# Lightning attention into a PReLU feed-forward: another hand-written list for the stretch ahead of the loop

## The chip, the cores and the metric

The kernel runs on one core of a Trainium2 chip. The metric is the time of one execution on the device, in microseconds (us), as the median of several runs. PE is TensorE (PEld its weight loads), DVE is VectorE, ACT is ScalarE, POOL is GpSimd, and SP issues most of the DMA transfers.

## What is computed

Block attention with a decaying state, per batch and head, and a feed-forward layer with a PReLU behind it. In the reference, cut to what matters:

```python
# q, k, v: (4, 8, 768, 64); lam: (8,); w_in: (512, 2048); w_out: (2048, 512); alpha: (2048,)
for b in range(nb):                       # blocks of 64 rows
    intra = (qb @ kb.T * Dmask) @ vb      # Dmask[i, j] = lam**(i - j) for i >= j, else 0
    inter = (qb * lam**(i + 1)) @ kv_state
    out[b] = intra + inter
    kv_state = lam**64 * kv_state + (kb * lam**(63 - i)).T @ vb
x = out as (3072, 512)
h = x @ w_in
g = max(h, 0) + alpha * min(h, 0)
y = g @ w_out                             # (3072, 512), float32
```

## The kernel before

**Tiles.** The kernel uses blocks of 128 rows, two of them at a time (a window of 256 rows). A *chunk* `c` of 0 to 5 is one window of two batches: chunk 0 is the first window of batches 0 and 1, chunk 1 the first window of batches 2 and 3, chunk 2 the second window of batches 0 and 1, and so on. A chunk has four *units*, numbered through from 0 to 23: unit `4c + 2 bi + hh` is batch `bi` of the chunk and four of the eight heads (`hh`). Each unit's state depends on that of the unit eight numbers before it, which has the same batch and heads, so units of one chunk are independent of each other.

**What a unit needs.** Its k, q and v arrive in float32 (`load`, issued on SP; chunk 0 in 256 KB halves of heads, later chunks in 512 KB). `cast` makes float16 copies, on ACT ("A"), DVE ("V") or POOL ("G"). `key_decayed` makes keys times decay. q and k are transposed, either on PE with a copy from PSUM behind it (`transposed` for one of the two, `transposes` for both with one copy of 1024 elements), or by a DMA transpose (`transposes(..., "D")`, issued on SP). `decayed` multiplies transposed queries by decay; in the first two chunks only the second block needs it.

**Clusters.** `cluster(old, new)` issues on PE: the state part of unit `old` (L361), the scores of unit `new` (L378), the masked scores times v of `old` (L390) and the state products of `new` (L405). Then DVE makes the masked scores of `new` (`sm`, L416), the outputs of `old` are copied into `xT` (the feed-forward's input), and the states of `new` are written: for the first block by ACT (L436, L437), for others by DVE (`R`, L440). From chunk 2 on POOL copies states into a block-diagonal tile `RD` (L454), which L361 reads. Outputs and state products share the one PSUM tile `acc` (two banks).

**Feed-forward.** `up(c, f)` computes one of 16 slices of h for a chunk (four matmuls of 512 columns, L465), then ACT makes relu(-h) (L473, tile `m`) and DVE the sum g (L489). With `bi` given it does half a chunk. `down(c, t, part, 4)` does a quarter of the 16 matmuls of an output tile (L502); behind the last quarter, ACT copies the tile (L515) and SP stores it (L518). The PSUM banks are `acc` (2), the scores `s0`, `s1` (1 each), and four that `up`, `down`, `fill` and PE transposes share under the tags "h" (a ring of two), "op" and "tk".

**Weights.** `load_win(i)` and `load_wout(i)` fetch the weights of 512 of the 2048 hidden columns each (four slices f); they are issued on POOL's queue, in its order. `gate(i, which)` is a one-element DMA on SP that reads from a weight piece, so SP issues nothing further until that piece has landed.

**Order.** Nothing is scheduled by the compiler: each engine runs what the program issues to it in the order of issue. Up to the loop this order is a list written out call by call (L573 to L788). `fill(n, bank)` issues n matmuls whose result nobody reads. From L790 on, the loop weaves `up(c)` and `down(c - 1)` for chunks 2 to 5 with the attention of the next chunk, and `down_last` ends the kernel.

Of the kernel before, what the change touches and what calls it, by code (L numbers as in the profile page):

```python
# [11 lines left out]
def kernel(  # L12
# [16 lines left out]
    nc = tc.nc  # L29
# [85 lines left out]
    def zero_states(batches, eng):  # L115
        for b in batches:
            for hh in (1, 0):
                eng.memset(RD[b, hh].bitcast(fp32), 0.0)
# [227 lines left out]
    def cluster(old, new, eng="A"):  # L346
# [5 lines left out]
        kv = [acc[:, a, 256:384].rearrange("p (h d) -> p h d", h=2) for a in range(2)]  # L352
        if old is not None:
            co, bo, ho = units[old]
            pbo, bb = co // 2, 2 * (co % 2) + bo
            to = T[old]
            for a in range(2):
                if 2 * pbo + a == 0:
                    continue
                for hp in range(2):  # L360
                    nc.tensor.matmul(  # L361
                        ot[a][:, hp, :].rearrange("p (e j) -> p e j", e=2),
                        lhsT=RD[bb, ho][:, a, hp].rearrange("p h d -> p (h d)"),
                        rhs=to["qdT"][:, :, hp, ds(a * 64, 64)],
                        start=(hp == 0),
                        stop=False,
                        skip_group_check=True,
                    )
# [29 lines left out]
        if new is not None:  # L398
            kv_of = [a for a in range(2) if 2 * pb + a + 1 < S // L]
            for hp in range(2):  # L400
                for e in range(2):
                    for hl in range(2):
                        for a in kv_of:
                            p = ds(a * 64, 64)
                            nc.tensor.matmul(  # L405
                                kv[a][ds(hl * 64, 64), hp, :],
                                lhsT=t["kdec"][p, e, 2 * hp + hl, :],
                                rhs=t["v16"][p, e, 2 * hp + hl, :],
                                start=(old is None and hp == 0 and e == 0),
                                stop=(e == 1),  # L410
                                skip_group_check=True,
                            )
# [7 lines left out]
        if old is not None:  # L420
# [8 lines left out]
        if new is not None:  # L429
            for a in kv_of:  # L430
                n = 2 * pb + a
                then = R[b, hh, n + 1]
                if n == 0:
# [3 lines left out]
                    nc.scalar.activation(then, kv[a], AF.Copy)  # L437
                    continue
                for hp in range(2):
                    nc.vector.scalar_tensor_tensor(  # L440
                        out=then[:, hp],
# [54 lines left out]
    def down(c, t, part, nparts, bank="op"):  # L496
# [12 lines left out]
        if part == nparts - 1:  # L509
            store(c, t, o_ps, 0, DM)  # L510
            del O[c, t]

    def store(c, t, o_ps, c0, n):
# [4 lines left out]
        nc.sync.dma_start(out=rows, in_=o_sb[:, 0:n])  # L518
# [53 lines left out]

    mask_logs(1)  # L573
    mask_logs(2)
    decay_mask(1)
    mask_logs(0)
    load(0, 0, "k", 0)
    load(0, 0, "q", 0)
    query_decay(2, 1)
    load(0, 0, "v", 0)  # L580
    load(0, 0, "k", 1)
    cast(0, "q16", "V")
    query_decay(0, 1)
    key_decay()
    key_decayed(1, "G")
    key_decayed(0, "G")
    mask_logs(3)
    query_decay(3, 1)
    cast(0, "v16", "A")
    decay_mask(3)  # L590
    cast(0, "k16", "V")
    fill(9, "h")
    transposed(0, 1, "V", "tk")
    cast(1, "k16", "A")
    fill(3, "h")
    transposed(1, 1, "V", "h")
    load(0, 0, "q", 1)
    cast(1, "q16", "A")
    transposed(0, 0, "V", "op")
    load(0, 0, "v", 1)  # L600
    query_decay(1, 1)
    decayed(0, "V")
    load(0, 1, "k", 0)
    load(0, 1, "q", 0)
    load(0, 1, "v", 0)
    cast(1, "v16", "G")
    state_decay()
    load(0, 1, "k", 1)
    decay_mask(0)
    fill(3, "tk")  # L610
    cluster(None, 0)
    slopes()
    transposed(1, 0, "V", "h")
    load_win(0)
    cast(2, "q16", "A")
    fill(5, "tk")
    transposed(2, 0, "V", "op")
    load(0, 1, "q", 1)
    cast(2, "k16", "A")
    cast(3, "k16", "V")  # L620
    load(0, 1, "v", 1)
    decay_mask(2)
    cluster(0, 1, "A")
    fill(4, "tk")
    transposed(3, 1, "V", "op")
    transposed(2, 1, "A", "tk")
    key_decayed(3, "V")
    load_win(1)
    key_decayed(2, "G")
    cast(3, "q16", "A")  # L630
    decayed(1, "G")
    fill(3, "h")
    cluster(1, None, "A")
    gate(1, "in")
    load(1, 0, "k", None)
    load(1, 0, "q", None)
    cast(2, "v16", "V")
    load(1, 0, "v", None)
    cluster(None, 2)
    transposed(3, 0, "A", "op")  # L640
    decayed(3, "V")
    cast(3, "v16", "V")
    decayed(2, "G")
    fill(4, "h")
    cluster(2, 3, "A")
    up(0, 0, 0, "tk")
    load_win(2)
    load_win(3)
    up(0, 1, 0, "h")
    fill(2, "op")  # L650
    cluster(3, None, "A")
    up(0, 5, 0, "h")
    up(0, 5, 1, "op")
    up(0, 3, None, "tk")
    up(0, 0, 1, "h")
    up(0, 2, None, "op")
    query_decay(3, 0)
    cast(4, "k16", "G")
    up(0, 6, None, "h")
    up(0, 9, None, "h")  # L660
    key_decayed(4, "G")
    up(0, 4, None, "tk")
    up(0, 1, 1, "op")
    up(0, 7, None, "h")
    transposed(4, 1, "V", "h")
    cast(5, "q16", "A")
    up(0, 14, None, "tk")
    transposed(5, 0, "A", "h")
    cast(4, "q16", "G")
    transposed(4, 0, "V", "h")  # L670
    gate(3, "in")
    load(1, 1, "k", None)
    load(1, 1, "q", None)
    cast(5, "k16", "G")
    decayed(5, "G")
    cast(4, "v16", "A")
    up(0, 12, None, "op")
    up(0, 8, None, "tk")
    load(1, 1, "v", None)
    up(0, 11, 0, "h")  # L680
    load_wout(0)
    cast(6, "k16", "A")
    up(0, 11, 1, "h")
    load_wout(1)
    gate(1, "out")
    key_decayed(5, "G")
    cast(7, "k16", "G")
    up(0, 15, None, "op")
    cluster(None, 4)
    load(2, 0, "k", None)  # L690
    load(2, 0, "q", None)
    load(2, 0, "v", None)
    load(2, 1, "k", None)
    transposed(5, 1, "A", "tk")
    cast(6, "q16", "A")
    up(0, 10, None, "h")
    up(0, 13, None, "tk")
    transposed(6, 1, "V", "h")
    transposed(6, 0, "A", "op")
    cast(5, "v16", "G")  # L700
    decayed(4, "G")
    cluster(4, 5, "A")
    transposed(7, 1, "V", "h")
    cast(7, "q16", "G")
    transposed(7, 0, "A", "op")
    down(0, 2, 0, 4, "tk")
    down(0, 3, 0, 4, "h")
    down(0, 0, 0, 4, "op")
    load_wout(2)
    key_decayed(6, "V")  # L710
    load_wout(3)
    decayed(6, "V")
    key_decayed(7, "G")
    query_decay(2, 0)
    cast(6, "v16", "A")
    cluster(5, 6, "A")
    cast(7, "v16", "A")
    down(0, 2, 1, 4, "tk")
    down(0, 0, 1, 4, "op")
    cast(9, "k16", "G")  # L720
    decayed(7, "V")
    down(0, 3, 1, 4, "h")
    cast(8, "q16", "G")
    cast(8, "v16", "G")
    cluster(6, 7, "A")
    cast(8, "k16", "V")
    transposes(8, "D", False)
    key_decayed(8, "V")
    down(0, 2, 2, 4, "tk")
    cast(11, "k16", "G")  # L730
    key_decayed(9, "G")
    load(2, 1, "q", None)
    load(2, 1, "v", None)
    down(0, 0, 2, 4, "op")
    query_decay(1, 0)
    key_decayed(10, "G")
    cluster(7, None, "A")
    cast(9, "q16", "G")
    transposes(9, "D", False)
    down(0, 3, 2, 4, "h")  # L740
    down(0, 3, 3, 4, "h")
    up(1, 12, None, "h")
    up(1, 1, None, "h")
    down(0, 0, 3, 4, "op")
    query_decay(0, 0)
    decayed(8, "G")
    up(1, 0, None, "h")
    up(1, 8, None, "h")
    down(0, 2, 3, 4, "tk")
    cast(10, "k16", "A")  # L750
    cluster(None, 8)
    up(1, 11, None, "op")
    cast(10, "q16", "A")
    up(1, 14, None, "tk")
    up(1, 13, None, "h")
    transposes(10, "D", False)
    up(1, 6, None, "h")
    down(0, 1, 0, 4, "op")
    decayed(9, "G")
    cast(9, "v16", "A")  # L760
    cast(11, "q16", "G")
    transposes(11, "D", False)
    cluster(8, 9, "V")
    up(1, 7, None, "h")
    key_decayed(11, "G")
    cast(11, "v16", "A")
    decayed(10, "G")
    down(0, 1, 1, 4, "op")
    down(0, 1, 2, 4, "op")
    cast(10, "v16", "A")  # L770
    cluster(9, 10, "V")
    load(3, 0, "k", None)
    up(1, 5, None, "tk")
    load(3, 0, "q", None)
    load(3, 0, "v", None)
    decayed(11, "G")
    up(1, 9, None, "h")
    down(0, 1, 3, 4, "op")
    load(3, 1, "k", None)
    load(3, 1, "q", None)  # L780
    load(3, 1, "v", None)
    cluster(10, 11, "V")
    up(1, 3, None, "tk")
    up(1, 2, None, "h")
    up(1, 15, None, "h")
    up(1, 4, None, "op")
    cluster(11, None, "A")
    up(1, 10, None, "tk")  # L788
# [42 lines left out]
```

## Time and profile before

| what | value |
|---|---|
| three runs | 219.31, 220.54, 218.2 us; median 219.31 |
| the profiled execution | 220.27 us, its span 218.5 us |
| PE busy | 207.5 us (95%) |
| DVE, ACT, POOL busy | 131.0, 115.8, 91.0 us |
| granted clock of PE | 0.997 on the mean |
| read from and written to HBM | 27.27 and 6.29 MB |

The span is the time between the first and the last instruction of the profiled execution. An engine's busy time is the sum over the time in which it ran an instruction; waiting, and issuing of DMA transfers on SP, are not busy. Idle time of an engine matters only where something else waits for what it does next. Durations used below are those of this one execution.

### The profile page before, as it was taken

The numbers are of one execution on the slowest core, as the hardware profiler recorded it, in microseconds if no ns is written. First come the engines' busy times: TensorE is split into PE (matmuls) and PEld (weight loads), VectorE is DVE, ScalarE is ACT, GpSimd is POOL, SyncE is SP. The second block draws the span as 40 slices with busy tenths as digits, with TensorE's granted clock in tenths as the row PEclk, the third lists the DMA queues.
The fourth block names the chain that finished last, engine by engine and source line by source line (L and its number), as shares of the span: only waits on it lengthen the run. The fifth ranks groups of instructions, "written<-read, shape, count | busy, mean of one in ns | idle before, by whom it ended". The sixth has DMA issues, their size and how long they took to land.

```text
span 218.5 us, 5235 instructions
## 1 busy us (share of the span) xinstructions
PE 207.5 (95%) x2087; PEld 105.9 (48%) x2087; DVE 131.0 (60%) x259; ACT 115.8 (53%) x224; POOL 91.0 (42%) x165
## 2 busy tenths in 40 slices
PE   7888999999898999999999999999999999999993
PEld 2445555644354544555545544554545444444453
DVE  7798688964697964866855646546645444444000
ACT  6876679764663575365456445545435434444121
POOL 5590059402587573697693484375331000000000
PEclk9999999999999999999999999999999999999998
DMA  5999999999899999689656997242111011110212
GB/s 151 295 245 189 264 290 217 165 228 242 201 270 197 308 234 212 160 211 240 168 123 193 155 237 221 55 99 65 33 51 48 0 51 50 48 48 3 96 48 96
DMA packets 62478, 33.90 MB, mean 155 GB/s; under 512 B 18150, under 2 KB 59510, under 8 KB 62454
## 3 DMA queue, kind: packets, MB, share of 16 engines
q1 hardware_dynamic: 58182, 29.37, 53.3%
q0 software_dynamic: 4224, 4.19, 12.3%
q8 instruction: 16, 0.26, 0.5%
q14 instruction: 8, 0.07, 0.1%
q10 hardware_dynamic: 48, 0.01, 0.0%
HBM read 27.27 MB, written 6.29 MB: 154 GB/s over the span
## 4 chain that ended last, share of the span: by engine, by line
PE 75%; DMA 12%; POOL 3%; SPq 3%; ACT 2%; issue 1%; DVE 1%; ACTq 0%; POOLq 0%
PE h_ps L465 34%; PE o_ps L502 27%; PE o_ps L525 6%; DMA w_out_sb<-in_moe_w_out_dram 6%; DMA qkT<-qk 4%; SPq L87 3%; PE s L378 3%; DMA kraw<-in_k_dram 3%; PE acc L390 2%; PE acc L361 2%; PE acc L405 1%; POOL w_out_sb L102 1%; POOL qk L248 1%; ACT xT L244 1%; ACT m L473 1%
## 5 line engine op out<-in xcount | busy, mean ns | idle before, releaser
L489 DVE SCALAR_TENSOR_TENSOR g<-m,oma,h_ps 128x512 f16<-128x512 f32 (+1 forms) x100 | 71.7, 725 | 59.1 <-ACT m L473 57.7
L465 PE MATMUL h_ps<-xT,w_in_sb 128*128 128x512 f16 (+1 forms) x400 | 95.6, 371 | 0.3 <-ACT qkT L244 0.3
L473 ACT ACTIVATE m<-h_ps 128x512 f32<-128x512 f32 (+1 forms) x100 | 57.5, 579 | 63.7 <-PE h_ps L465 62.2
L502 PE MATMUL o_ps<-w_out_sb,g 128*128 128x512 f16 x320 | 81.3, 380 | 0.3 <-DMA w_out_sb<-in_moe_w_out_dram 0.3
L465 PEld LDWEIGHTS <-w_in_sb 128*128 128x128 f16 x400 | 38.1, 98 | 42.0 <-issue 0.6
L502 PEld LDWEIGHTS <-g 128*128 128x128 f16 x320 | 30.3, 98 | 35.7 <-issue 0.6
L454 POOL COPY RD<-R 64x128 f16<-64x128 f16 x64 | 18.5, 288 | 38.2 <-DVE R L440 36.5
L416 DVE TENSOR_TENSOR sm<-s,dmask 128x512 f16<-128x512 f32 x48 | 30.8, 684 | 4.2 <-PE s L378 4.0
L336 POOL TENSOR_TENSOR qdT<-qkT,qdecay 128x512 f16<-128x512 f16 (+1 forms) x20 | 21.4, 1071 | 6.7 <-DMA qkT<-qk 4.4
L515 ACT ACTIVATE o_sb<-o_ps 128x512 f32<-128x512 f32 (+2 forms) x26 | 14.7, 564 | 17.6 <-PE o_ps L525 10.9
L274 POOL TENSOR_TENSOR kdec<-kraw,kdecay 128x512 f16<-128x512 f32 x21 | 21.9, 1046 | 4.0 <-DMA kraw<-in_k_dram 3.9
L248 POOL CAST qk<-kraw 128x512 f16<-128x512 f32 x17 | 10.5, 618 | 24.7 <-DMA kraw<-in_k_dram 12.2
L244 ACT ACTIVATE xT<-acc 128x512 f16<-128x512 f32 x21 | 12.5, 597 | 14.3 <-PE acc L405 11.0
L440 DVE SCALAR_TENSOR_TENSOR R<-R,rdecay,acc 128x64 f16<-128x64 f16 x64 | 14.2, 275 | 1.6 <-ACT R L437 1.6
L525 PE MATMUL o_ps<-w_out_sb,g 128*128 128x512 f16 (+2 forms) x96 | 14.1, 308 | 0.0
L378 PE MATMUL s<-qkT 64*64 64x128 f16 x384 | 10.0, 222 | 2.2 <-DMA qkT<-qk 2.2
L244 ACT ACTIVATE qk<-qraw 128x512 f16<-128x512 f32 x18 | 11.2, 624 | 0.4 <-DMA qraw<-in_q_dram 0.4
L525 PEld LDWEIGHTS <-g 128*128 128x128 f16 x96 | 8.1, 98 | 6.1
L361 PE MATMUL acc<-qdT,RD 128*128 128x128 f16 x80 | 8.5, 219 | 1.6 <-DVE R L440 1.0
L361 PEld LDWEIGHTS <-RD 128*128 128x128 f16 x80 | 6.1, 97 | 7.9 <-ACT qkT L244 1.7
L248 POOL CAST v<-vraw 128x512 f16<-128x512 f32 x15 | 9.3, 621 | 1.2 <-ACT qdecay L229 1.2
L390 PE MATMUL acc<-sm,v 64*64 64x128 f16 x384 | 9.6, 218 | 0.0
(57 smaller groups left out, 109.1 us busy)
## 6 DMA issues: line engine op xcount, KB each, us to landing
out_dram<-o_sb SPq DMA_DIRECT2D x23, 256.0 KB, 2.0
kraw<-in_k_dram SPq DMA_DIRECT2D x10, 512.0 KB, 5.5
qraw<-in_q_dram SPq DMA_DIRECT2D x10, 512.0 KB, 5.8
vraw<-in_v_dram SPq DMA_DIRECT2D x10, 512.0 KB, 5.6
w_in_sb<-in_moe_w_in_dram POOLq DMA_DIRECT2D x4, 512.0 KB, 8.0
w_out_sb<-in_moe_w_out_dram POOLq DMA_DIRECT2D x4, 512.0 KB, 7.9
kraw<-in_k_dram SPq DMA_DIRECT2D x4, 256.0 KB, 5.4
qraw<-in_q_dram SPq DMA_DIRECT2D x4, 256.0 KB, 5.3
```

Of the source, the lines that this page charges most:

```text
L244: nc.scalar.activation(out, in_, AF.Copy)
L248: nc.gpsimd.tensor_copy(out=out, in_=in_)
L274: engine(eng).tensor_tensor(out=kdec, in0=kr, in1=kdecay[:, ds(4 * hh, 4), :].rearrange("p h e -> p e h").unsqueeze(3).to_broadcast([128, ...
L336: engine(eng).tensor_tensor(out=qdT[:, :, :, p], in0=(t["qps"] if eng == "P" else t["qkT"][:, 0])[:, :, :, p], in1=qdecay[:, hh, :, :, p], ...
L361: nc.tensor.matmul(ot[a][:, hp, :].rearrange("p (e j) -> p e j", e=2), lhsT=RD[bb, ho][:, a, hp].rearrange("p h d -> p (h d)"), rhs=to["qd ...
L416: nc.vector.tensor_tensor(out=sm, in0=s[hl], in1=mask_of(hl, hh), op=ALU.mult)
L454: nc.gpsimd.tensor_copy(out=RD[b, hh][p, a, :, hl, :], in_=R[b, hh, 2 * pb + a][p])
L465: nc.tensor.matmul(h_ps[:, 0:n] if bi is None else h_ps[:, 0:n].rearrange("p (e j) -> p e j", e=2), lhsT=w_in_sb[:, gi, ts(f, 128)], rhs=x ...
L473: nc.scalar.activation(m[:, 0:n], h_ps[:, 0:n], AF.Relu, scale=-1.0)
L489: nc.vector.scalar_tensor_tensor(out=g, in0=mv, scalar=oma[:, f : f + 1], in1=hv, op0=ALU.mult, op1=ALU.add)
L502: nc.tensor.matmul(o_ps, lhsT=lhs(c, f, t), rhs=w_out_sb[:, f, :], start=(f == 0), stop=(f == NF - 1),)
L525: nc.tensor.matmul(o_ps[:, 0:n], lhsT=lhs(c, f, t), rhs=w_out_sb[:, f, ds(x, n)], start=(f == 0), stop=(f == NF - 1),)
```

## The change

The list up to the loop is replaced by another. `cluster` gets two options: with `own`, the state products of a unit go into two banks of the "h" ring instead of into `acc`, and with `state_first`, the states of `new` are written before the outputs of `old` are copied. `down(..., hold)` leaves the store for a later `store_held`. `up(..., later)`, which was there, leaves the product for a later `slope_product`. `slopes` takes its bank from "op" instead of "h". The units of chunk 0 go in the order 0, 2, 1, 3. The loop is unchanged.

```diff
-    def cluster(old, new, eng="A"):
+    def cluster(old, new, eng="A", state_first=False, own=False):
...
+        if own:
+            kv = [bank_of("h", "kv")[:, 0:128].rearrange("p (h d) -> p h d", h=2) for a in range(2)]
...
-                                start=(old is None and hp == 0 and e == 0),
+                                start=((own or old is None) and hp == 0 and e == 0),
...
-        if old is not None:
+        def output():
...
-        if new is not None:
+        def state():
...
+        if old is not None and not state_first:
+            output()
+        if new is not None:
+            state()
+        if old is not None and state_first:
+            output()
...
-        at = h_ps_pool.tile([128, CH], fp32, tag="h", name="at_ps")
+        at = bank_of("op", "at_ps")
...
-        nc.sync.dma_start(out=rows, in_=o_sb[:, 0:n])
+        HELD[c, t] = (rows, o_sb[:, 0:n])
+        if not hold:
+            store_held(c, t)
+
+    def store_held(c, t):
+        rows, tile = HELD.pop((c, t))
+        nc.sync.dma_start(out=rows, in_=tile)
```

The new list, several calls to a line:

```python
query_decay(1, 1); key_decay(); query_decay(0, 1); mask_logs(0); mask_logs(1); decay_mask(1); mask_logs(3)
mask_logs(2); load(0, 0, "k", 0); cast(0, "k16", "G"); key_decayed(0, "V"); load(0, 0, "q", 0)
cast(0, "q16", "G"); fill(4, "h"); transposes(0, "A", False); load(0, 0, "k", 1); load(0, 0, "q", 1)
cast(1, "q16", "A"); load(0, 1, "q", 0); decayed(0, "V"); cast(2, "q16", "V"); key_decayed(1, "V")
load(0, 1, "k", 0); cast(2, "k16", "V"); cast(1, "k16", "G"); query_decay(2, 1); query_decay(0, 0)
query_decay(3, 1); load(0, 0, "v", 0); cast(0, "v16", "G"); key_decayed(2, "V"); decay_mask(0)
fill(5, "h"); transposes(1, "A", False); load_win(0); load(0, 1, "q", 1); cast(3, "q16", "G")
fill(5, "op"); transposed(2, 1, "V", "h"); transposed(2, 0, "A", "op"); decay_mask(3); state_decay()
cluster(None, 0, own=True); slopes(); load(0, 1, "v", 0); cast(2, "v16", "A"); load_win(1); fill(4, "h")
cluster(0, 2, "A", own=True); load(0, 1, "k", 1); cast(3, "k16", "G"); load(0, 0, "v", 1); decayed(2, "G")
cast(1, "v16", "A"); load(0, 1, "v", 1); fill(2, "tk"); transposes(3, "V", False); decay_mask(2)
cluster(2, 1, "A", own=True); cast(3, "v16", "A"); decayed(1, "G"); fill(4, "tk"); cluster(1, None, "A")
load(1, 0, "q", None); decayed(3, "G"); key_decayed(3, "G"); cluster(None, 3, own=True); load_win(2)
gate(1, "in"); load(1, 0, "k", None); load_win(3); query_decay(3, 0); fill(3, "op"); cluster(3, None, "A")
up(0, 0, 0, "tk"); load(1, 0, "v", None); cast(4, "k16", "G"); load(1, 1, "k", None); load_wout(0)
load(1, 1, "q", None); up(0, 0, 1, "h", True); slope_product(0, 0, 1); up(0, 1, None, "op")
up(0, 4, None, "tk", True); slope_product(0, 4, None); up(0, 3, None, "h", True); key_decayed(4, "G")
slope_product(0, 3, None); cast(5, "k16", "G"); up(0, 6, None, "h", True); up(0, 2, None, "op")
up(0, 7, None, "tk"); slope_product(0, 6, None); cast(4, "q16", "A"); up(0, 5, None, "h")
up(0, 8, None, "op"); up(0, 11, None, "tk"); up(0, 10, None, "h"); load_wout(1); cast(4, "v16", "A")
gate(3, "in"); up(0, 14, None, "h"); up(0, 15, None, "op"); up(0, 13, None, "h")
transposes(4, "V", False); decayed(4, "P"); gate(1, "out"); up(0, 9, None, "h"); up(0, 12, None, "op")
cluster(None, 4); cast(5, "q16", "G"); transposes(5, "A", False); down(0, 0, 0, 4, "h")
load(1, 1, "v", None); down(0, 3, 0, 4, "h"); cast(6, "k16", "G"); down(0, 2, 0, 4, "op")
cast(6, "q16", "V"); load_wout(2); transposes(6, "A", False); key_decayed(5, "G"); down(0, 0, 1, 4, "h")
load(2, 0, "k", None); cast(5, "v16", "V"); key_decayed(6, "V"); cast(7, "q16", "A")
down(0, 2, 1, 4, "op"); decayed(6, "G"); load(2, 0, "q", None); cast(7, "k16", "V"); load_wout(3)
cluster(4, 5, "V", state_first=True); load(2, 1, "k", None); cast(8, "q16", "G")
transposes(7, "A", False); decayed(5, "V"); down(0, 3, 1, 4, "h"); down(0, 3, 2, 4, "h")
cast(9, "q16", "G"); cast(6, "v16", "V"); down(0, 2, 2, 4, "op"); decayed(7, "V")
cluster(5, 6, "A", state_first=True); key_decayed(8, "G"); down(0, 1, 0, 4, "tk"); down(0, 1, 1, 4, "tk")
down(0, 1, 2, 4, "tk"); key_decayed(7, "V"); load(2, 0, "v", None); cast(8, "k16", "V")
key_decayed(9, "V"); transposes(8, "D", False); cast(9, "v16", "G"); cast(7, "v16", "A")
cluster(6, 7, "V", state_first=True); down(0, 0, 2, 4, "h"); down(0, 0, 3, 4, "h"); key_decayed(10, "V")
cast(9, "k16", "G"); load(2, 1, "q", None); down(0, 2, 3, 4, "op", True); cluster(7, None, "A")
cast(8, "v16", "V"); transposes(9, "D", False); cast(10, "k16", "G"); down(0, 3, 3, 4, "h", True)
up(1, 0, None, "h"); query_decay(1, 0); store_held(0, 3); decayed(8, "G"); up(1, 12, None, "op", True)
slope_product(1, 12, None); up(1, 6, None, "h", True); slope_product(1, 6, None); load(2, 1, "v", None)
cluster(None, 8); key_decayed(11, "G"); query_decay(2, 0); decayed(9, "G"); up(1, 1, None, "h", True)
slope_product(1, 1, None); cast(11, "k16", "A"); up(1, 7, None, "op", True); cast(10, "q16", "A")
transposes(10, "D", False); slope_product(1, 7, None); cast(11, "q16", "A"); down(0, 1, 3, 4, "tk")
up(1, 13, None, "h", True); load(3, 0, "q", None); cluster(8, 9, "A"); transposes(11, "D", False)
slope_product(1, 13, None); load(3, 0, "k", None); decayed(10, "G"); up(1, 2, None, "tk", True)
slope_product(1, 2, None); up(1, 3, None, "op"); store_held(0, 2); cast(10, "v16", "A")
up(1, 15, None, "h", True); cluster(9, 10, "A"); slope_product(1, 15, None); up(1, 10, None, "tk", True)
load(3, 0, "v", None); cast(11, "v16", "A"); load(3, 1, "k", None); slope_product(1, 10, None)
up(1, 11, None, "h"); up(1, 9, None, "op", True); decayed(11, "G"); cluster(10, 11, "A")
up(1, 5, None, "tk"); up(1, 14, None, "h"); slope_product(1, 9, None); up(1, 4, None, "h", True)
slope_product(1, 4, None); cluster(11, None, "A"); load(3, 1, "v", None); load(3, 1, "q", None)
up(1, 8, None, "tk")
```

More of the change, by code (lines that the diff above doesn't have):

```diff
@@ L605 @@
[L605 to L620, printed above, removed]
+    load(0, 1, "q", 0)
+    decayed(0, "V")
+    cast(2, "q16", "V")
+    key_decayed(1, "V")
+    load(0, 1, "k", 0)
+    cast(2, "k16", "V")
@@ new lines @@
+    cast(1, "k16", "G")
+    query_decay(2, 1)
+    query_decay(0, 0)
+    query_decay(3, 1)
+    load(0, 0, "v", 0)
+    cast(0, "v16", "G")
+    key_decayed(2, "V")
+    decay_mask(0)
+    fill(5, "h")
+    transposes(1, "A", False)
+    load_win(0)
+    load(0, 1, "q", 1)
+    cast(3, "q16", "G")
+    fill(5, "op")
+    transposed(2, 1, "V", "h")
+    transposed(2, 0, "A", "op")
+    decay_mask(3)
+    state_decay()
+    cluster(None, 0, own=True)
+    slopes()
+    load(0, 1, "v", 0)
+    cast(2, "v16", "A")
@@ L666 @@
[L666 to L676, printed above, removed]
+    load_win(3)
+    query_decay(3, 0)
+    fill(3, "op")
+    cluster(3, None, "A")
+    up(0, 0, 0, "tk")
+    load(1, 0, "v", None)
+    cast(4, "k16", "G")
+    load(1, 1, "k", None)
+    load_wout(0)
+    load(1, 1, "q", None)
@@ L717 @@
[L717 to L752, printed above, removed]
+    cast(5, "v16", "V")
+    key_decayed(6, "V")
+    cast(7, "q16", "A")
+    down(0, 2, 1, 4, "op")
@@ L773 @@
-    up(1, 5, None, "tk")
[L774 to L779, printed above, removed]
-    load(3, 1, "q", None)
[L781 to L788, printed above, removed]
+    slope_product(1, 7, None)
+    cast(11, "q16", "A")
+    down(0, 1, 3, 4, "tk")
```

271 lines of the change are left out of this document (154 added, 117 removed).

## The prediction

> **What bounds the kernel now.** The first view is the table of stretches; the columns are the stretch, its length, then busy time (instructions) of PE, PEld, DVE, ACT and POOL, the granted clock, the DMA share and GB/s.
>
> ```profile
> 22.84:35.00 12.16, 11.88 (x80) 6.79 (x75) 8.86 (x16) 9.54 (x20) 5.11 (x8) 1.00 1.15 281
> 35.00:51.00 16.00, 15.48 (x268) 8.58 (x266) 11.93 (x27) 11.18 (x29) 5.73 (x8) 1.00 1.14 205
> 51.00:58.50 7.50, 6.24 (x29) 2.63 (x27) 4.43 (x6) 4.75 (x9) 2.86 (x5) 1.00 0.81 181
> 58.50:78.20 19.70, 18.42 (x273) 9.87 (x274) 17.20 (x38) 9.97 (x18) 15.05 (x28) 1.00 1.09 268
> ...
> 90.00:120.00 30.00, 30.00 (x361) 15.65 (x360) 19.73 (x41) 16.70 (x29) 23.15 (x43) 1.00 0.74 178
> 120.00:150.00 30.00, 30.00 (x298) 15.25 (x296) 17.52 (x31) 15.21 (x26) 15.99 (x30) 1.00 0.62 141
> ```
>
> From the loop's first matmul (78.2 us in the timeline) PE is never idle, and the change does not touch that code. So the time is the loop's start plus a fixed 140.3 us, plus 1.8 us around the span (220.27 - 218.5). From 22.84, where matmuls run solid, to 78.2, PE works 52.03 of 55.36 us: 3.33 us of waits are all that a better order there can win. What they wait for, in PE's waits up to 80 us (columns: who, for whom, total, times, longest):
>
> ```profile
> PE s L378 <- DMA qkT<-qk: 2.2, 3, 1.0
> ...
> PE acc L361 <- DVE R L440: 1.0, 3, 0.4
> PE acc L361 <- ACT m L473: 0.6, 1, 0.6
> PE acc L405 <- ACT xT L244: 0.5, 1, 0.5
> PE o_ps L502 <- DMA w_out_sb<-in_moe_w_out_dram: 0.3, 1, 0.3
> ```
>
> DMA transposes that came late are the largest item, 2.2 us, with one weight piece 0.3. The rest of the start is hand-overs in the recurrence of units 0 to 3. VectorE comes next: in the last stretch before the loop it is busy 17.2 of 19.7 us, and its groups there are
>
> ```profile
> L489 DVE SCALAR_TENSOR_TENSOR g<-m,oma,h_ps 128x512 f16<-128x512 f32 x11 | 7.8, 746 | 0.2
> L416 DVE TENSOR_TENSOR sm<-s,dmask 128x512 f16<-128x512 f32 x8 | 5.2, 686 | 2.7 <-PE s L378 2.7
> L440 DVE SCALAR_TENSOR_TENSOR R<-R,rdecay,acc 128x64 f16<-128x64 f16 x16 | 3.4, 276 | 0.0
> L246 DVE CAST xT<-acc 128x512 f16<-128x512 f32 x3 | 2.0, 682 | 0.0
> ```
>
> Nearly all its idle time, 2.7 us, is waiting for scores that wait for DMA transposes.
>
> **The first 23 us.** The bytes are the same; v of unit 0 goes from third to seventh 256 KB load. By landing place (3.73, 4.63, 6.49, 7.75, 9.56 for the 1st, 2nd, 3rd, 4th, 6th; 11.36 for the 8th) that is 6.5 to about 10.4 us. POOL casts it (0.6 us), so unit 0's state products run at 11.4 to 11.7 instead of 10.0 to 10.3: 1.4 us late. What follows, from ACT's timeline (start, length):
>
> ```profile
> 10.38 0.55 ACT L436 ACTIVATE RD<-acc 64x128 f16<-64x128 f32 x2 [0.27 <-PE acc L405]
> 10.94 0.28 ACT L437 ACTIVATE R<-acc 128x128 f16<-128x128 f32 x1
> 11.39 0.63 ACT L244 ACTIVATE qk<-qraw 128x512 f16<-128x512 f32 x1 [0.17 <-DMA qraw<-in_q_dram]
> 11.92 0.61 ACT L244 ACTIVATE qk<-kraw 128x512 f16<-128x512 f32 x1
> 12.44 0.51 ACT L207 ACTIVATE dmask<-dmask 128x384 f32<-128x384 f32 x1
> 13.34 0.60 ACT L244 ACTIVATE xT<-acc 128x512 f16<-128x512 f32 x1 [0.39 <-PE acc L405]
> 13.83 0.54 ACT L436 ACTIVATE RD<-acc 64x128 f16<-64x128 f32 x2
> ```
>
> Instructions that follow one another start 0.5 us apart where each takes 0.6. ACT now has two copies of 1024 elements in one instruction; the trace has none. Below: 0.6, one copy of 512; above: 1.2, two of them. I take 0.95, as 256 elements cost 0.38 and 512 cost 0.60. With five query decays (0.3), key decays 0.4, three mask exponentials (0.43), a cast, a copy and the wait for q of unit 1 (7.75), ACT reaches state 0 at 12.2 and ends it at 13.0. The state products now lie in the two banks "h", and the list's next fill takes an "h" bank: four filler matmuls of 0.25 us wait behind that copy (cover for it: none), to 14.1. Cluster (0,2) has unit 0's outputs by 14.8. From there the three further units pass in turn through ACT (xT 0.5, state 0.83, v cast 0.53) and DVE (masked scores 1.29 a unit, states 0.46, a 1024 copy 0.75): xT of unit 3 ends at about 21.9, bounds 21.6 and 22.4 (every instruction at its full length). Solid matmuls from 22.0, against 22.84; but only one half up-projection is done by then, not two (0.48 us). Gain 0.3, bounds -0.1 and 0.8. The own banks for states 0 to 3 let a unit's states be made while its predecessor's outputs are still in "acc": the 0.5 us row of L405 is worth that much at most and is inside this walk.
>
> **22 to 58 us.** PE's work: before had 12 whole and 6 half ups left (0.864 and 0.48 each), now 15 and 1, so 52.03 + 0.2 = 52.2 us; transposes, downs and clusters are as many as before. With no wait at all the loop would start at 74.2. The waits:
> - Up stage: each up needs 0.6 on ACT and 0.75 on DVE for 0.86 on PE, four banks in turn. Before lost 0.28 in 12 us; I take 0.3. `later` and `hold` only move ends behind other instructions of the list.
> - Weights. w_in pieces took 2.3 to 3.3 us each and a 512 KB load 1.8. One more load (q of chunk 1) now goes ahead of the gate, so the second w_in lands at about 21.9, not 19.9, and the gate lets k of chunk 1 go 1.8 us later. POOL issues w_in 2 and 3 at 19.3, behind unit 3's key decay, not at 14.8; they land by 27.5, first needed at about 28. POOL's next cast waits for k (29), w_out 0 is issued behind it, w_out 1 at 32.3, and by bytes they land at 37.2 and 39.9. PE wants them at 37.2 and 40.4: no margin. Queued behind w_out 1 on SP's gate: v of unit 6 (issued 40.6, lands at 45.5 by the 5 us of such loads; wanted at 46), then k and q of chunk 2. Stall between 0 and 4.0 us: the upper end if the rate of 41.5 to 57.6 (two w_out at 2.7 and four loads at 1.8, 12.6 us of transfers, in 16.1) holds from the gate on. I take 0.5, nearer the lower end, as transfers up to 41.47 kept the full rate.
>
> The Trainium skill (DMA: Bandwidth & Descriptors, section "Queues, rings and completion order") says that each DMA engine takes packets from its queue rows in turn. By that w_out 0, on another queue than the chunk's loads, would not stand behind them and would land some 2 us sooner, with a stall of 0. The rows are against it early (loads on SP landed every 0.87 us through 14.86 though the first w_in had been issued at 10.64) and for it later (k issued at 42.12 landed at 52.31, beside two w_out pieces).
>
> - DMA transposes of units 8 to 11 took 3.7 us from issue to landing. Their casts now stand so that they are issued about 51.5, 56, 61.5 and 64, and wanted at 58, 62, 65.5 and 69. The 2.2 us of waiting goes, with 0.3 to 2 us of margin each.
>
> **58 us to the loop.** Here 13 ups and one down are left where before had 12 ups and four downs, so DVE gets less time: PE's work is 16.4 us. DVE has, up to the last states, one old product (0.75), four pairs of masked scores 5.2, 16 states 3.4, 8 products at the 0.68 at which they follow each other 5.4: 14.7 us, started 1.0 after the stage. Each cluster waits for the states of the one before it. Then POOL's copy 0.6, cluster 0.7, one up 0.86: 17.7 us, 1.3 over PE's work. What moved xT of units 8 to 10 from DVE to ACT (2.0 us) is in this count; left on DVE it would be 19.7.
>
> **Sum.** 74.2 + 0.3 + 0.5 + 1.3 = 76.3 for the loop's start, 78.2 before: 1.9 us less. Profiled: span 216.6, time 218.4. The profiled execution is 1.0 over the median of 219.31, so against the median 217.4. The three runs differ by 1.1%, so about 1% is what can be told from no change.
>
> **Rivals.**
> - All waits hidden: DVE's lag runs on into the loop, where an up and a down share 1.73 us, and the weights are in time. For it: up to three products may be pending before a bank is missed. Against it: clusters need the states, not the products. Gain 0.3 + 3.3: 215.7.
> - Late weights (slower than before). The chain k, POOL cast, w_out 0, w_out 1, SP's gate, v of unit 6: the upper end above, 4.0 us in place of 0.5, and v of unit 6 slowed at the same rate (5 to 6.4 us, some 0.8 of it uncovered) make the loop start at 80.6: 221.7. It decides from 2.4 us of such stalls on. For it: the 16.1 us row and the missing margin. Against it: the full rate before 41 us, and that the loads are 1.8 us fewer by then.
> - Nothing left: the later first state and the fill behind it cost an early 1.5 us more than I count (1.9 becomes 0.4), because ACT and DVE hand over at full length and POOL's casts share time with DVE (0.80 instead of 0.61 in one row). Then 218.9.
>
> **Chances.** Forecast 0.50 (own range 216.2 to 218.7), all hidden 0.26, nothing left 0.11, late weights 0.13. Faster by over 1% is below 217.1: the second case and a third of the first, 0.43. Slower by over 1% is above 221.5: most of the late weights, 0.10. Within: 0.47. Range 215.4 to 220.6.
>
> **What would show it.** Right: PE solid from about 22; waits for qkT by DMA gone from PE's list; DVE busy over 80% of the last 18 us ahead of the loop with clusters waiting for states (L443, L457); the loop at 76.3. Wrong: waits for w_out or v of unit 6 over 1 us; filler matmuls waiting long for "h" with xT of unit 3 past 23; or a last stretch with no wait.

## The result: 0.8% faster, and what the profile after shows

The changed kernel takes 217.51 us on the median of 20 executions (216.17 to 220.27), the kernel before 219.2 (218.2 to 220.78) on the same chip. The ratio is 0.9922, 95% interval 0.9896 to 0.9948, so 1.7 us less. Two of the 20 executions, 219.86 and 220.27 us, ran in a slower state at a granted clock of 0.992 and are not in the ratio. The profiled execution is 218.6 us with a span of 216.8, 1.1 us above its median, as that of before was (220.27 against 219.2). The two profiles can be set side by side: their spans differ by 1.7 us.

The same table of stretches, from where matmuls run solid (without the gaps of the hand-overs in units 0 to 3) to the loop:

```profile
20.74:35.50 14.76, 14.67 (x81) 7.05 (x76) 10.75 (x17) 10.37 (x19) 5.52 (x9) 1.00 1.12 231
35.50:51.00 15.50, 14.32 (x252) 8.52 (x252) 11.84 (x27) 7.54 (x16) 2.44 (x3) 1.00 1.13 214
51.00:58.35 7.35, 6.84 (x46) 2.92 (x45) 4.02 (x8) 4.89 (x11) 3.08 (x5) 1.00 1.10 228
58.35:76.50 18.15, 16.44 (x265) 9.10 (x266) 16.79 (x39) 12.62 (x24) 12.43 (x26) 1.00 1.12 262
```

Solid matmuls begin at 20.74 instead of 22.84. From there to the loop PE works 52.29 of 55.76 us, so it waits 3.5 us; before it worked 52.03 of 55.36 and waited 3.3. The 2.1 us are not a lead of 2.1 us: at 22.84 the kernel before had two half up-projections behind it (8 matmuls at 20.18), the changed kernel has none at 20.74. The loop starts at 76.5 instead of 78.2, and from there both kernels need 140.3 us. The whole gain of this pair of profiles thus stands ahead of 21 us, and a better order of the rest seems to have won nothing. What PE waits for in that stretch (columns as before):

```profile
PE s L380 <- DMA qkT<-qk: 2.1, 2, 1.7
PE o_ps L514 <- DMA w_out_sb<-in_moe_w_out_dram: 1.1, 1, 1.1
```

These are all its waits of note. The hand-overs among engines are gone, but the two kinds of transfer that were late before are still late: DMA transposes 2.1 us (2.2 before), a weight piece 1.1 (0.3 before). DVE's groups from 58.35 to 76.5:

```profile
L499 DVE SCALAR_TENSOR_TENSOR g<-m,oma,h_ps 128x512 f16<-128x512 f32 x15 | 10.3, 743 | 0.0
L418 DVE TENSOR_TENSOR sm<-s,dmask 128x512 f16<-128x512 f32 x8 | 5.1, 685 | 1.4 <-PE s L380 1.4
L443 DVE SCALAR_TENSOR_TENSOR R<-R,rdecay,acc 128x64 f16<-128x64 f16 x16 | 3.4, 276 | 0.0
```

DVE is busy 16.8 of 18.15 us, yet its only idle time is again for scores that wait for a transpose, and no cluster on PE waits for its states.

### The profile page after: what moved, and what is told of

Its sections match the earlier page's. It is cut to its first block, busy times and chain, and to the rows that moved or that the text cites. A ratio compares the mean times of both kernels' runs of the same rounds, so it can differ in the third digit from the quotient of the medians.

```text
span 216.8 us, 5184 instructions
## 1 busy us (share of the span) xinstructions
PE 206.6 (95%) x2069; PEld 105.4 (49%) x2069; DVE 129.5 (60%) x254; ACT 115.6 (53%) x218; POOL 87.7 (40%) x163
## 4 chain that ended last, share of the span: by engine, by line
PE 69%; DMA 23%; POOL 3%; SPq 2%; issue 1%; ACT 1%; POOLq 0%; ACTq 0%
PE h_ps L475 29%; PE o_ps L514 28%; DMA w_out_sb<-in_moe_w_out_dram 8%; PE o_ps L543 6%; DMA qkT<-qk 5%; DMA w_in_sb<-in_moe_w_in_dram 4%; DMA kraw<-in_k_dram 4%; DMA vraw<-in_v_dram 3%; PE s L380 2%; PE acc L392 2%; PE acc L363 1%; SPq L87 1%; POOL qk L248 1%; POOL qdT L336 1%; PE acc L407 1%
## 5 line engine op out<-in xcount | busy, mean ns | idle before, releaser
L499 DVE SCALAR_TENSOR_TENSOR g<-m,oma,h_ps 128x512 f16<-128x512 f32 (+1 forms) x97 | 70.4, 741 | 57.7 <-ACT m L483 57.0
L475 PEld LDWEIGHTS <-w_in_sb 128*128 128x128 f16 x388 | 37.1, 98 | 43.2 <-issue 0.2
L244 ACT ACTIVATE xT<-acc 128x512 f16<-128x512 f32 x22 | 13.1, 597 | 11.9 <-PE acc L407 8.7
L274 POOL TENSOR_TENSOR kdec<-kraw,kdecay 128x512 f16<-128x512 f32 x17 | 17.8, 1045 | 0.1
L248 POOL CAST qk<-kraw 128x512 f16<-128x512 f32 x20 | 12.1, 610 | 12.0 <-DMA kraw<-in_k_dram 11.3
L443 DVE SCALAR_TENSOR_TENSOR R<-R,rdecay,acc 128x64 f16<-128x64 f16 x56 | 12.4, 275 | 0.0
L244 ACT ACTIVATE qk<-qraw 128x512 f16<-128x512 f32 x17 | 10.5, 623 | 0.1
L137 PE MATMUL unread<-ident 128*128 128x512 f16 x27 | 8.7, 452 | 1.2 <-ACT R L440 1.0
L380 PEld LDWEIGHTS <-qkT 64*64 64x64 f16 x384 | 6.2, 106 | 6.5 <-DMA qkT<-qk 2.8
```

Of the source, the lines that this page charges most:

```text
L244: nc.scalar.activation(out, in_, AF.Copy)
L248: nc.gpsimd.tensor_copy(out=out, in_=in_)
L274: engine(eng).tensor_tensor(out=kdec, in0=kr, in1=kdecay[:, ds(4 * hh, 4), :].rearrange("p h e -> p e h").unsqueeze(3).to_broadcast([128, ...
L380: nc.tensor.matmul(s[hl][ds(a * 64, 64), hp, 1 - e, :].rearrange("p (e j) -> p e j", e=2), lhsT=t["qkT"][p, 1, e, hp, ds(a * 64, 64)], rhs ...
L475: nc.tensor.matmul(h_ps[:, 0:n] if bi is None else h_ps[:, 0:n].rearrange("p (e j) -> p e j", e=2), lhsT=w_in_sb[:, gi, ts(f, 128)], rhs=x ...
L499: nc.vector.scalar_tensor_tensor(out=g, in0=mv, scalar=oma[:, f : f + 1], in1=hv, op0=ALU.mult, op1=ALU.add)
```

## The experiments

All ratios are to the kernel before, run in turn on the same chip, with 95% intervals; the changed kernel's is 0.9922 (0.9896 to 0.9948). Two kernels whose intervals overlap widely are not told apart. A profile shows one execution, and executions of the changed kernel lie up to 1.3% apart (216.17 to 219.04 us at a granted clock of 0.997 to 1.000), so profiles of two variants need not rank as their medians do: that of h1_first is the fastest of its twelve (218.27 us), that of the changed kernel is 1.1 us above its median. What a profile below shows is thus what one execution waited for, not what an edit is worth.

**Which part of the list holds the gain?** Two hybrids: the new list up to the end of unit 3 with the old list behind it (h1_first), and the reverse (h2_rest).

```diff
 # h1_first
     ... new list
     cluster(3, None, "A")
     up(0, 0, 0, "tk")
-    ... new list from here
+    ... old list from here, without what is issued already
```

> The changed list up to the cluster that ends unit 3, then the list of before from its first up-projection on (order of units 0, 2, 1, 3 and the own banks kept; the calls that the first part has already issued are left out). Theory A (the first 21 us hold the whole gain, the rest of the list is a wash with 3.4 us of PE waits on either side): solid matmuls from 20.7 us, loop from 76.5, ratio 0.990 to 0.994. Rival B (bytes: weights and loads land when they land, so a list of before's kind, started 1.1 us sooner, waits 1.1 us longer for w_out and for DMA transposes): PE's waits after 21 us rise from 3.4 to 4.5, loop from 77.5 to 78.2, ratio 0.996 to 1.000.

> The list of before up to its last cluster of unit 3 (with two half up-projections and w_in 2 and 3 there), then the changed list from its first whole up-projection on. Theory A (gain sits in the first 21 us): solid from 22.8, PE's waits behind it 3 to 4 us, loop from 78, ratio 0.998 to 1.003. Rival C (the rest of the new list is the better one, but its gain is hidden by waits of bytes that a later start takes away): the wait for w_out of 1.1 us and for the transposes of unit 10 shrink to under 1.5 us together, loop from 76.5, ratio 0.992 to 0.995.

Measured: h1_first 218.98 us, 0.9984 (0.9959 to 1.0009). h2_rest 218.15 us, 0.9947 (0.9919 to 0.9976). Theory A falls on both: the first part by itself gives nothing that can be told, though its profile shows the first up-projection at 20.5; the rest by itself gives 0.5%. The pair of profiles above had misled: waits of the same sum do not mean that the order behind them is worth the same. A likely reason, not shown, is that the new rest was started 2 us sooner and had the same arrivals to wait for. PE's longest waits in h1_first after 20.5 us:

```profile
PE s L380 <- DMA qkT<-qk: 1.3, 1, 1.3
PE tpx L322 <- POOL qk L248: 1.2, 1, 1.2
...
```

The second is new: the old rest wants k of unit 4 at 28.5 us, and POOL's cast of it ends at 29.7, when its load is in. That is a wait of the kind that rival B named, for k in place of w_out. But of B only the ratio came out: its sum of waits (4.5 us) and its loop (77.5 to 78.2) did not. This execution waited 3.0 us in all, and its span of 216.5 us puts the loop at 76.2. Where the other eleven lose the lead is not shown. The profile of h2_rest is of an execution 2.6 us above its median, so which waits the new rest saves is not shown either.

**Does the early lead count?** Three parts of the change were undone or altered one by one.

```diff
 # no_own
-    cluster(None, 0, own=True)
+    cluster(None, 0)                      # and so in all four
 # v_third
     load(0, 0, "q", 0)
+    load(0, 0, "v", 0)
...
-    load(0, 0, "v", 0)
 # units0123: units 1 and 2 changed places in the first part, with their
 # loads, casts and transposes; decay_mask(2) moved ahead of its cluster
-    cluster(0, 2, "A", own=True)
+    cluster(0, 1, "A", own=True)
...
-    cluster(2, 1, "A", own=True)
+    cluster(1, 2, "A", own=True)
```

> The changed list with the state products of chunk 0 back in the tile of the outputs. Theory (own banks let a unit's states be made beside its predecessor's outputs): each of the three following clusters waits for ACT's copy of the outputs, some 0.5 us each, solid matmuls from 21.5 to 22.3, ratio to the changed kernel 1.003 to 1.007. Rival (the own banks buy nothing: the four filler matmuls that stood behind ACT's copy of state 0 run at once, and the masked scores on DVE set the pace): solid from 20.2 to 20.8, ratio to the changed kernel 0.997 to 1.000.

> One part of the change undone: v of unit 0 is the third load again, ahead of k and q of units 1 and 2, everything else as in the changed list. Theory J (k and q first feeds the transposes of units 1 and 2 sooner): each of these four loads lands 0.9 us later, ACT and DVE casts with them; solid matmuls from 21.3 to 21.8 instead of 20.7, but as the bytes behind them set the pace from 21 to 41 us, the time moves by no more than 0.3 us, ratio to the changed kernel 0.999 to 1.002. Rival K (the early lead counts in full): ratio to the changed kernel 1.003 to 1.005. Rival L (v's cast held POOL for 3.1 us and w_in 0 behind it, so v sooner is better): 0.996 to 0.999.

> The changed list with units 1 and 2 of chunk 0 changed places in its first part, loads, casts, transposes and clusters alike, and the mask exponential that unit 1 needs moved ahead of its cluster: the order is 0, 1, 2, 3. Theory M (the order of units is neutral by itself, as the units of a chunk have the same work; only the mask's 0.43 us on ACT comes earlier): solid matmuls from 20.7 to 21.3, ratio to the changed kernel 0.999 to 1.002. Rival N (0, 2, 1, 3 is what allows the early start, as units 0 and 2 share masks and query decays): solid 0.8 us or more later, ratio 1.002 to 1.005.

| kernel | solid matmuls from | w_in 2 issued | median us | ratio |
|---|---|---|---|---|
| changed | 20.7 | 18.0 | 217.51 | 0.9922 (0.9896 to 0.9948) |
| no_own | 22.6 | 18.0 | 218.09 | 0.9928 (0.9903 to 0.9952) |
| v_third | 22.1 | 19.3 | 218.4 | 0.9973 (0.9946 to 1.0000) |
| units0123 | 21.0 | 18.7 | 218.02 | 0.9950 (0.9922 to 0.9978) |

Without the own banks the solid part begins 1.8 us later, more than was expected, and the time moves by 0.0006 of the whole in the ratio, by 0.6 us between the medians, not told from nothing. In its profile the lead is not missed: the changed kernel, with it, waits 1.1 us for w_out 0 and 2.1 for DMA transposes, no_own not at all for w_out 0, 0.3 for a later piece and 2.0 for a transpose. v as third load begins only 1.3 us later and costs more, 0.005 (rival K by size, though the intervals still touch). The third column goes with the cost: with v third w_in 2 and 3 are issued 1.3 us later. That this is the cause is not shown: in the profile of v_third w_out 1 and v of unit 6 landed no later (40.6 and 45.7 us, against 40.7 and 46.0), and that execution took 218.05 us, less than the changed kernel's profiled one. units0123 lies between, not told from the changed kernel; whether the order of units matters by itself stays open.

**Is w_out late by its place in POOL's queue, or by bytes?**

```diff
 # wout_first
     load(1, 0, "v", None)
+    load_wout(0)
     cast(4, "k16", "G")
...
-    load_wout(0)
```

> One edit of the changed list: w_out 0 is issued on POOL ahead of the cast that waits for k of chunk 1, so at about 19.6 us instead of 30.5. Theory I (order on POOL's queue made w_out 0 late): it lands by 32, the wait of 1.1 us at the first down goes, loop 1.0 us sooner, ratio to the changed kernel 0.994 to 0.997. Rival B (bytes): its 2.7 us of transfer now stand ahead of k, v of unit 4 and all behind them; ACT's cast of v of unit 4 (31.7 us, waiting 0.5 us already) holds the relus behind it 2 us longer, PE waits there 1 to 2.5 us instead, ratio to the changed kernel 1.000 to 1.006.

Measured: 219.19 us, 0.9986 (0.9955 to 1.0016); the gain is gone. Both answers hold a part. w_out 0 was issued at 20.1 and landed at 32.8, but v of unit 4 landed at 34.8 instead of 31.6. ACT's timeline from 30 us (start, length, what ended the idle time):

```profile
30.82 0.60 ACT L483 ACTIVATE m<-h_ps 128x512 f32<-128x512 f32 x1 [0.27 <-PE h_ps L475]
34.85 0.63 ACT L244 ACTIVATE v<-vraw 128x512 f16<-128x512 f32 x1 [3.44 <-DMA vraw<-in_v_dram]
35.39 1.55 ACT L483 ACTIVATE m<-h_ps 128x512 f32<-128x512 f32 x3
```

One cast of v stands 3.4 us in ACT's queue, three relus wait behind it, and PE stands 2.4 us for a bank (its wait list has h_ps, ended by DVE's g). That is rival B as it was written down: a piece taken forward puts the one behind it back. The wait for w_out 0 itself did go, as theory I said.

**Then are the DMA engines ever less busy there?** The table of stretches for single microseconds, the last figures being the DMA share and GB/s, of the changed kernel (the share adds up the times of packets, so it passes 1 where they overlap):

```profile
20.00:21.00 1.00, 0.91 (x21) 0.60 (x20) 0.73 (x3) 0.54 (x3) 0.00 (x0) 1.00 1.05 155
21.00:22.00 1.00, 1.00 (x10) 0.72 (x8) 0.19 (x1) 0.86 (x3) 0.00 (x0) 1.00 1.23 205
```

There is one dip between 10 and 26 us, at 20 to 21, and POOL's timeline shows what was missing. (The share is low again from 31 to 35 us, 0.93 to 1.10, and from 40 to 44, 0.92 to 1.09; what bounds the transfers there was not tried by an edit of its own.)

```profile
13.37 1.31 POOL L336 TENSOR_TENSOR qdT<-qkT,qdecay 128x256 f16<-128x256 f16 x2
16.40 0.67 POOL L336 TENSOR_TENSOR qdT<-qkT,qdecay 128x256 f16<-128x256 f16 x1 [1.73 <-DVE qkT L246]
17.04 1.04 POOL L274 TENSOR_TENSOR kdec<-kraw,kdecay 128x512 f16<-128x512 f32 x1
18.03 1.54 POOL L96 DMA_DIRECT2D w_in_sb<-in_moe_w_in_dram  x2
29.95 0.61 POOL L248 CAST qk<-kraw 128x512 f16<-128x512 f32 x1 [10.38 <-DMA kraw<-in_k_dram]
```

POOL stands 1.7 us for unit 3's transposed queries, and the issue of w_in 2 and 3 is queued behind that. Before, they were issued at 14.8.

```diff
 # win_early
     decayed(1, "G")
+    load_win(2)
+    load_win(3)
...
-    load_win(2)
...
-    load_win(3)
```

> One edit of the changed list: w_in 2 and 3 are issued on POOL two instructions sooner, ahead of the products of unit 3 for which POOL stands idle from 14.7 to 16.4 us: at 14.7 instead of 18.0. In the changed kernel w_in 1 landed at 21.15 and w_in 2 at 25.27, 4.1 us for a transfer that takes 2.7. Theory O (the DMA engines set the pace from 21 to some 60 us, and ran dry for about 1.4 us there): w_in 2 lands by 24, w_out 0 and 1 and all behind them about 1 us sooner, loop 0.7 to 1.2 us sooner, ratio to the changed kernel 0.994 to 0.997, ratio to before 0.986 to 0.989. Rival P (waits come from the order of hand-overs, not from bytes): landings move, the loop does not; ratio to the changed kernel 0.999 to 1.001.

Measured: 216.78 us, 0.9863 (0.9831 to 0.9894), as theory O said. w_in 2 is issued at 14.8, lands at 24.6 (25.3 before the edit), w_in 3 at 27.1 (28.7), k's cast is done 1.0 us sooner, v of unit 6 lands at 44.9 (46.0), and the dip has gone:

```profile
20.00:21.00 1.00, 0.91 (x20) 0.56 (x20) 0.77 (x3) 0.54 (x3) 0.00 (x0) 1.00 1.25 207
```

On its POOL timeline the two pieces are issued ahead of the wait:

```profile
14.76 1.54 POOL L96 DMA_DIRECT2D w_in_sb<-in_moe_w_in_dram  x2
16.54 0.67 POOL L336 TENSOR_TENSOR qdT<-qkT,qdecay 128x256 f16<-128x256 f16 x1 [0.24 <-DVE qkT L246]
```

What PE waits for in this execution from 20.5 us to the loop:

```profile
PE o_ps L514 <- DMA w_out_sb<-in_moe_w_out_dram: 1.2, 1, 1.2
PE s L380 <- DMA qkT<-qk: 1.0, 2, 0.7
```

Theory O's size came out, and the loads landed 1.1 us sooner as it said; w_out 0 did not (37.5 instead of 37.7), and PE waits as long for it as before the edit. The 1.1 us that this profile saves are waits for DMA transposes, 1.0 instead of 2.1.

> The edit of win_early, and the state products of chunk 0 back in the tile of the outputs. With w_in late, taking the own banks away cost 0.5 us of time though matmuls ran solid 1.8 us later. Theory O (the early lead was worth little because the transfers came no sooner): with the transfers sooner the own banks count for more, 1.0 to 1.8 us; ratio to before 0.991 to 0.995, against 0.987 for win_early. Rival Q (the own banks are worth 0.5 us whatever the transfers do): within 0.003 of win_early.

Measured: 218.01 us, 0.9921 (0.9890 to 0.9951). With w_in sooner, taking the own banks away costs 1.2 us (216.78 to 218.01); the two intervals just overlap, 0.9890 against 0.9894. The same edit cost 0.6 us between the medians with w_in late, but in the ratios 0.0058 here against 0.0006 there. This is the direction theory O gave, that a lead on PE is worth what the transfers behind it allow; with intervals this wide it is likely and not certain.

**The filler that waits, and both edits.**

```diff
 # fill_tk
-    fill(4, "h")
+    fill(4, "tk")
     cluster(0, 2, "A", own=True)
```

> One edit of the changed list: the four filler matmuls ahead of the second cluster use the bank tk instead of a bank of the ring in which state products 0 lie. The wait of 1.0 us for ACT's copy of state 0 (filler, 11.1 to 12.1 us) goes. Theory D (the chain of the first 21 us hangs on that wait): second cluster at 12.0 instead of 13.0, solid from about 20.0, and the loop from 75.9 or, if weights by bytes take it back at the first down, from 76.5 with the wait for w_out up from 1.1 to 1.8 us. Rival E (the casts of v on ACT and the copies on DVE set the pace anyway): solid from 20.6 to 20.8, nothing gained.

> The edit of win_early and that of fill_tk together (w_in 2 and 3 two instructions sooner on POOL; four filler matmuls in bank tk instead of h). Theory O: the two gains are of one kind, as fill_tk's too came with w_in 2 issued 0.5 us sooner, so they add only in part: ratio to before 0.982 to 0.987. Rival (they add in full): 0.978 to 0.982. Rival P: as fill_tk alone, 0.988.

Measured: fill_tk 216.87 us, 0.9885 (0.9846 to 0.9923); win_early_tk 216.41 us, 0.9861 (0.9827 to 0.9896). In fill_tk the filler's 1.0 us wait for ACT is gone, but solid matmuls begin at 20.9, not sooner (rival E on that point). w_in 2 was issued at 17.5. That it is faster than the changed kernel is likely and not certain (the intervals overlap), and that fill_tk adds to win_early is not shown. win_early and win_early_tk have the lowest medians of this study, 1.4% below the kernel before. In the profile of win_early_tk PE has only one wait from 20.66 to the loop at 73.8:

```profile
20.66:36.00 15.34, 15.34 (x121) 7.86 (x117) 11.87 (x19) 11.26 (x21) 6.60 (x9) 1.00 1.20 249
36.00:55.91 19.91, 19.91 (x260) 10.60 (x258) 14.91 (x34) 11.27 (x25) 4.60 (x7) 1.00 1.09 228
55.91:73.83 17.92, 16.39 (x265) 9.04 (x265) 16.64 (x39) 12.95 (x24) 12.09 (x25) 1.00 1.11 265
```

It is 1.53 us, for the DMA transpose of unit 10.

**Why is that transpose late?** In the changed kernel it was issued at 62.15 and landed at 67.95. One edit puts v of chunk 2's second batch ahead of the transpose of unit 9; another, on win_early_tk, puts the half of that v which unit 11 needs behind the transpose of unit 10.

```diff
 # v21_early
     load(2, 1, "q", None)
+    load(2, 1, "v", None)
...
-    load(2, 1, "v", None)
 # v21_halves (on win_early_tk)
-    load(2, 1, "v", None)
+    load(2, 1, "v", 0)
...
     transposes(10, "D", False)
+    load(2, 1, "v", 1)
```

> One edit of the changed list: the second 512 KB v of chunk 2 is issued on SP directly behind its q (some 56.9 us) instead of behind the DMA transpose of unit 9 and a store (60.8 us). In the changed kernel the transpose of unit 10 was issued at 62.15 and landed at 67.95, 5.8 us where unit 9's took 3.1, and PE waited 1.7 us for it. Theory F (unit 10's transpose stood behind v's bytes): it now lands in 3 to 4 us, by 66, that wait goes; unit 9's lands some 0.5 us later, with at most 0.5 us of waiting; loop 1.2 us sooner, ratio to the changed kernel 0.993 to 0.996. Rival G (the last stretch is bound by DVE, as the prediction had it: 14.7 us of work before the last states): the wait goes but clusters wait for states instead; at most 0.4 us gained. Rival H (DMA transposes simply vary between executions): the wait stays of 0.5 to 2 us.

> The two edits of win_early_tk, and the second v of chunk 2 (512 KB, ahead of the DMA transpose of unit 10 on SP) in two halves of heads: the half that unit 10 needs stays, the half of unit 11 goes behind that transpose. In win_early_tk the transpose of unit 10 was issued at 59.7 and landed at 65.3, and PE waited 1.53 us for it, its only wait up to the loop. Theory F (it stood behind v's bytes; moving all of v ahead only shifted the wait to units 8 and 9): it lands 0.9 us sooner, the wait falls to 0.6 or less and no other takes its place; ratio to before 0.981 to 0.984. Rival R (something ahead of v in the queue sets it: q of chunk 2, 512 KB issued some 5 us before): wait unchanged, ratio 0.986.

Measured: v21_early 217.39 us, 0.9920 (0.9889 to 0.9951), the same as the changed kernel. The issues on SP there (start, length of the issue):

```profile
53.69 1.50 SPq L292 DMA_TRANSPOSE qkT<-qk  x1
...
56.34 0.71 SPq L87 DMA_DIRECT2D vraw<-in_v_dram  x1
58.72 2.97 SPq L292 DMA_TRANSPOSE qkT<-qk  x1
...
63.39 1.24 SPq L292 DMA_TRANSPOSE qkT<-qk  x1
```

Unit 10's transpose, now with nothing large in front, landed in 3.1 us (66.5) and was not waited for; in the nine kernels here that have v in front of it, it took 4.6 to 6.1. But unit 9's, now directly behind that v, was issued at 58.7, and PE waited 0.6 us for it, till 64.5, 5.8 us after the issue (3.1 to 4.8 us to landing in the nine). So theory F's mechanism holds, but the wait moved. PE also waited 1.1 us for unit 8's, which landed in 5.9 us (59.5). It was issued ahead of that v and took 3.6 to 6.7 us in the nine, so this wait is not shown to come from the edit.

v21_halves 217.03 us, 0.9893 (0.9867 to 0.9919): no better than win_early_tk. Unit 10's landed in 4.7 instead of 5.6 us and was waited for 0.6 us instead of 1.5, while PE waited 0.8 for unit 11's. Again the bytes in front of one transpose were moved in front of another, and neither theory F's ratio (0.981 to 0.984) nor rival R's unchanged wait came out. In this execution the granted clock was 0.92 from 20 to 36 us (1.00 in the changed kernel's), so its times ahead of 36 us can't be compared.

## Why the prediction was right

The forecast was 217.4 us and 1.9 us less; measured are 217.51 and 1.7. The loop was forecast from 76.3 and starts at 76.5; behind it the 140.3 us held. But the sum is right because two terms were wrong by much the same amount with opposite signs: without waits the loop would have started at 73.0 (20.74 + 52.29), not 74.2, and the waits were 3.5 us, not 2.1. That these two nearly cancel is luck. By the prediction's own signs the mechanism did not come out: solid from 20.74 and not 22, waits for DMA transposes not gone, no cluster waiting for states, and a wait for w_out over 1 us, which it had named as a sign of being wrong. DVE was busy over 80% of the last stretch, as it said.

The halves run crossed speak for its split all the same: it put 0.3 us on the first part and 1.6 on the rest, and by their ratios the first part alone is worth some 0.4 us (-0.2 to 0.9) and the rest alone 1.2 (0.5 to 1.8). Each part was there measured beside the old form of the other, so this and the pair of profiles need not agree; which waits the new rest saves there is not shown.

**The first 21 us** were mis-sized: "gain 0.3, bounds -0.1 and 0.8". Solid matmuls begin at 20.74, with no half up-projection done, where the walk had 22.0 with one done; xT of unit 3 ends at 21.45, just outside the bounds 21.6 to 22.4 that the walk gave. The hand-overs came in the order of the walk, at first 0.9 us sooner:

```profile
10.00 0.61 POOL L248 CAST v<-vraw 128x512 f16<-128x512 f32 x1 [3.10 <-DMA vraw<-in_v_dram]
...
11.24 0.54 ACT L439 ACTIVATE RD<-kv 64x128 f16<-64x128 f32 x2
...
12.12 1.02 PE L137 MATMUL unread<-ident 128*128 128x512 f16 x4 [0.98 <-ACT R L440]
```

ACT reaches state 0 at 11.24, where the walk had 12.2, and the filler matmuls wait for it till 12.1, where it had 13.0. The loads ran ahead of the landing places taken from before: q of unit 1 was there for its cast at 7.26 (walk: 7.75), v of unit 0 at 10.0 (10.4). The copy of 1024 elements, not in the trace of before, takes 1.00 on ACT, taken as 0.95; on DVE 0.68.

**Waits.** Forecast were 0.3 in the up stage (measured 0.1), 0.5 for weights and v of unit 6 (1.14, all for w_out 0), none for DMA transposes (2.14), and 1.3 for DVE ahead of the loop (none): 2.1 in all, 3.5 measured. The step "the 2.2 us of waiting goes" failed. Its issue times were right within 0.7 us for two of four and 2.3 and 2.9 us early for units 8 and 9 (forecast 51.5, 56, 61.5, 64; measured 53.8, 58.9, 62.15, 64.6). And it took 3.7 us to landing for every one, where unit 10's needed 5.8 behind 512 KB of v. The profile of before had the warning: there unit 10's, issued at 63.81, took 4.86, and PE waited 1.0 us for it. The step "Each cluster waits for the states of the one before it" failed too: from unit 8 to the loop no run here shows such a wait, also not win_early_tk and fill_tk, in which the transposes cost 1.5 and 0.6 us. Taking away transposes' 1.5 us, win_early_tk needs 16.4 us from unit 8's scores to the loop, PE's work and not the 17.7 forecast (the terms of that step, added again, give 17.9).

**Weights.** The step's chain held: w_in 1 at 21.15 (forecast 21.9), k's cast at 29.95 (29), w_out 0 at 37.7 and w_out 1 at 40.7 (37.2 and 39.9), v of unit 6 at 46.0 (45.5). The stall of 1.14 lies in the bounds of 0 to 4.0. By the Trainium skill's rule on DMA engines that take packets from their queues in turn (DMA: Bandwidth & Descriptors, "Queues, rings and completion order") the prediction's estimate was a stall of 0, with w_out 0 at some 35. It landed at 37.7, so here the rows of before that the sum went by were the better guide. wout_first doesn't decide between the two: w_out 0, issued at 20.1 and so ahead of v of unit 4, landed ahead of it at 32.8 and put it back by 3.2 us, as either would have it.

**The rivals.** "All waits hidden" had 215.7 (from the sum's own 74.2 it would be 215.3); even the best kernel here, at 216.41, does not reach it. "Late weights" had the right place and not the size. "Nothing left" was wrong about the start: it had the first part costing 1.5 us more, and it came out sooner than counted.

## What to carry to other kernels

Where the DMA engines are busy from the start and PE is 95% busy, expect a lead on the compute engines to be worth only what the arrivals behind it allow. Look for the microsecond in which the DMA share dips, and for the instruction that stood in front of the next issue on an in-order queue. Here, moving one transfer ahead of another moved the wait (wout_first, v21_early, v21_halves), and issuing the same transfers earlier, while POOL stood idle, removed 1.1 us of it in win_early's profile. Two profiles whose waits add up to the same do not show that their orders are equal: run the halves crossed. And a sum that comes out right is not yet a mechanism: compare it term by term.

## What the runs showed of the hardware that was not expected

- A DMA transpose of the same size landed 3.1, 4.5 or 5.8 us after its issue within one execution of the changed kernel. The 5.8 was behind a 512 KB load, and in v21_early, with that load moved, this transpose took 3.1 and the one now behind the load was waited for till 5.8 us after its issue.
- The issue of a 512 KB load took 0.4 to 0.7 us on SP at the head of a group of loads (k and v at 21.95 and 22.38 in the changed kernel) and up to 3.9 us (v at 45.86) behind others, so what stands behind it on SP can be issued later, not only served later: k at 23.11 took 3.3 us to issue, and q was issued at 26.47.
- At a granted clock of 0.997 to 1.000, executions of the changed kernel spread from 216.17 to 219.04 us, 1.3%; how far DMA speed makes this spread was not measured.
